# The last head pair's activations turned by TensorE instead of by the DMA, and one store per token block in the last chunk

## The chip, the cores and the metric

The kernel runs on one core of one Trainium2 chip. The metric is the device time of one execution in microseconds; the kernel before took 352.42 us (the median of three runs, 352.25 to 353.17). The profile shown further down is of one of these executions, with a span of 351.2 us and TensorE at its full clock throughout.

## What is computed

The reference is a causal attention with a forget gate for 8 batches of 8 heads, 576 tokens and head size 64, followed by a two-layer network with an exact GELU. The heads of one token, side by side, are its 512 inputs to the network.

```python
# attention: q, k, v (8, 8, 576, 64), f (8, 8, 576)
scores = scale * np.matmul(q, k.transpose(0, 1, 3, 2))
cum = np.cumsum(np.log(np.clip(f, 0.0001, 1.0)), axis=-1)
scores = np.where(causal, -1e9, scores + cum[:, :, :, None] - cum[:, :, None, :])
attn = softmax(scores)                      # written out in the reference
o = np.matmul(attn, v)
# network: x (4608, 512), w_in (512, 2048), w_out (2048, 512)
x = o.transpose(0, 2, 1, 3).reshape(B * S, H * D)
h = x @ w_in
g = 0.5 * h * (1.0 + erf(h / sqrt(2)))
out = g @ w_out                             # (4608, 512) f32
```

## The kernel before

The kernel works batch by batch. Of a batch's 576 tokens, 512 go through the network as a chunk of their own; the last 64 of every batch are gathered in `tails`, and these eight pieces make a ninth chunk, which is computed at the end. For a batch from 2 to 7 the stages are:

1. `attention(b)`: for each of four head pairs, four score tiles on TensorE, whose exponentials ScalarE takes. Between the score tiles, `take(fill, n)` puts n steps of the second matrix product of the batch before, so that TensorE has something to do while ScalarE works. `av(i)` multiplies the exponentials of pair i with v, and `normalize` writes `x` on VectorE.
2. `x`, which has tokens on the partitions, must be turned so that features lie on the partitions: `xT`. Batches 2 to 7 do this for each pair with one DMA transpose that SyncE issues (`x_dma`).
3. `gemm1(b, ffb)` multiplies a block of 128 columns of `w_in` with `xT` in four products (`kt` 0 to 3, one for each head pair), and ScalarE's GELU brings the result out of PSUM. There are 16 such blocks.

```python
    def to_xT(b, i, copy, pool=m_psum, tag="m", ps=None):      # on TensorE
        if ps is None:
            shape = [P, 2, 1024] if pool is s_psum else [P, XC]
            ps = pool.tile(shape, BF16, tag=tag, name="ps_x")
            if pool is s_psum:
                ps = ps[:, 0, 0:XC]
        for m in range(NBLK):                                  # NBLK = 5
            nc.tensor.transpose(
                ps[:, m * P : (m + 1) * P], x_of[b, i][:, m, :, :], ident_bf
            )
        copy(xT(b)[:, i, :], ps)

    def x_dma(b, i):                                           # by the DMA
        nc.sync.dma_start_transpose(
            xT(b)[:, i, :].rearrange("d (m p) -> d m p", p=P),
            x_of[b, i].rearrange("p m h d -> p (m h d)"),
        )

    def x_tail(b):
        nc.gpsimd.tensor_copy(tails[:, :, b * TL : (b + 1) * TL], xT(b)[:, :, XC - TL :])

    def gemm1(c, ffb, kts=range(4), ps=None, act=True):
        src = xT(c) if c < B else tails
        if ps is None:
            ps = m_psum.tile([P, TC], FP32, tag="m", name="ps1")
        for kt in kts:
            nc.tensor.matmul(ps, w_in_sb[:, kt, ffb * P : (ffb + 1) * P],
                             src[:, kt, 0:TC], start=(kt == 0), stop=(kt == n_dm - 1))
        if n_dm - 1 in kts and act:
            gelu(c, ffb, ps)                                   # ScalarE, g <- ps
        return ps
```

A step of the second product is either "n" (one product with all 128 rows of the array) or "r" (two products with 64 rows each, side by side). A plan has 64 steps for a batch.

```python
    PLAN = [
        (0, "o", 16 * "r"),
        (1, "m", 6 * "r" + "n" + 8 * "r" + "n"),
        (2, "m", 9 * "r" + "n" + 6 * "r"),
        (3, "s", 5 * "r" + 11 * "n"),
    ]
    # ... cut: PLAN_0, PLAN_1 (used in batch 2), gemm2_rows, which walks a plan ...

    FILL = [[7, 6, 3, 3], [1, 3, 3, 2], [1, 3, 3, 3], [1, 3, 3, 3], [6]]
    FILL_2 = [[8, 8, 8, 8], [8, 8, 4, 4], [4, 4, 4, 4], [4, 4, 4, 4], [6]]

    def attention(b):
        # ... cut: which fill ...
        for i in range(HP):                                    # HP = 4 head pairs
            for t in range(4):
                scores(b, i, t)
                take(fill, counts[i][t])
                if i and t == 1:
                    av(i - 1)
                    x_dma(b, i - 1)
                # ... cut: loads and transposes of the next batch's q, k, v ...
        take(fill, counts[HP][0])
        av(HP - 1)
        x_dma(b, HP - 1)
        take(fill, 999)                                        # what is left

        pss = [gemm1(b, ffb, (0, 1)) for ffb in range(2)]
        for ffb in range(2):
            gemm1(b, ffb, (2,), pss[ffb])
        more = s_psum.tile([P, 2, 512], FP32, tag="s", name="ps1")
        pss += [more[:, 0, :], more[:, 1, :]]
        gemm1(b, 2, (0, 1, 2), pss[2])
        for ffb in range(3):
            gemm1(b, ffb, (3,), pss[ffb])
        gemm1(b, 3, range(4), pss[3])
        if b + 1 < B:
            untangle(b + 1, 0)
            weigh_v(b + 1, 0)
        x_tail(b)

    # the main loop, after attention(b):
        for ffb in range(4, n_ff):                             # n_ff = 16
            gemm1(b, ffb)
            # ... cut: untangle (VectorE) and weigh_v (GpSimd) of the next batch ...
```

The first four blocks are thus ordered so that the products with the last pair (`kt` 3) come as late as they can. The pools `s_psum`, `o_psum` and `m_psum` have two buffers each; `more` is one buffer of `s_psum` with two banks.

The last chunk's stores (line 424) are made in `gemm2`, one for each batch that has 64 rows in the block of 128:

```python
                if c < B:
                    at = [(c * S + ts * P, 0, P)]
                else:
                    b0 = P // TL * ts
                    at = [(b * S + TC, (b - b0) * TL, TL) for b in range(b0, b0 + P // TL)]
                for row, p0, n in at:
                    (nc.scalar if p0 else nc.sync).dma_start(
                        out[row : row + n, c0:c1], ot[p0 : p0 + n, c0:c1]
                    )
```

Of the kernel before, what the change touches and what calls it, by code (L numbers as in the profile page):

```python
# [8 lines left out]
FP32 = mybir.dt.float32  # L9
# [5 lines left out]
P = 128  # L15
S = 576
D = 64
H = 8
HP = 4
NBLK = 5  # L20
K0 = [0, 128, 256, 384, 448]
TC = 512
# [30 lines left out]
def kernel(  # L53
# [10 lines left out]
    nc = tc.nc  # L64
    B = q.shape[0]
# [4 lines left out]
    n_ff = d_ff // P  # L70
    n_sub = TC // P
    XC = NBLK * P
    TL = S - TC
# [14 lines left out]
    s_psum = ctx.enter_context(tc.tile_pool(name="s_psum", bufs=2, space=PSUM))  # L88
    o_psum = ctx.enter_context(tc.tile_pool(name="o_psum", bufs=2, space=PSUM))
# [47 lines left out]
    for t, op, fill in (  # L137
# [4 lines left out]
            out=t[0:D],  # L142
            in_=t[0:D],
            compare_op=op,
            fill=fill,
# [89 lines left out]
    def untangle(b, i):  # L235

        for which, src in enumerate(tq_of[b]):
            for h in range(2):
                dst = (qT, kT)[which][i]
                rows = dst[h * D : (h + 1) * D, :].rearrange(  # L240
                    "d (p j two) -> d two p j", j=JT // 2, two=2
                )
                for odd in range(2):
                    nc.vector.tensor_copy(  # L244
                        rows[:, odd],
                        src[odd * D : (odd + 1) * D, 2 * i + h].rearrange(
                            "d j p -> d p j"
                        ),
                    )
# [3 lines left out]
    def weigh_v(b, i, eng=nc.gpsimd):  # L253

        if b not in vw_of:
            vw_of[b] = v_pool.tile([P, H, NBLK, D + 1], BF16, tag="vw", name=f"vw{b}")
        hs = slice(2 * i, 2 * i + 2)
        bh = b * H + 2 * i
        w = wT[:, :, bh : bh + 2].rearrange("p n h -> p h n")
        eng.tensor_tensor(  # L260
            vw_of[b][:, hs, :, 0:D],
            v_sb[:, hs, :, :],
            w.unsqueeze(3).to_broadcast([P, 2, NBLK, D]),
            Alu.mult,
        )
        eng.tensor_copy(vw_of[b][:, hs, :, D], w)
# [79 lines left out]
    def to_xT(b, i, copy, pool=m_psum, tag="m", ps=None):  # L346
# [5 lines that stand above are left out]
        for m in range(NBLK):  # L352
# [5 lines that stand above are left out]
    def x_dma(b, i):  # L358
# [7 lines that stand above are left out]
# [4 lines left out]
# [5 lines that stand above are left out]
            nc.tensor.matmul(  # L375
                ps,
                w_in_sb[:, kt, ffb * P : (ffb + 1) * P],
                src[:, kt, 0:TC],
                start=(kt == 0),
                stop=(kt == n_dm - 1),  # L380
            )
        if n_dm - 1 in kts and act:
            gelu(c, ffb, ps)
        return ps
# [9 lines left out]
    def gemm2(c):  # L394

        whole = (0, d_model)
        order = [(ts, kt, whole) for ts in range(n_sub) for kt in range(n_ff)]
        if c == B:
            order[-n_ff:] = [
                (n_sub - 1, kt, part)  # L400
                for part in ((0, 3 * P), (3 * P, d_model))
                for kt in range(n_ff)
            ]
        pss = {}
        for ts, kt, (c0, c1) in order:
            if kt == 0:
                pss[ts] = m_psum.tile([P, d_model], FP32, tag="m", name="ps2")
            nc.tensor.matmul(  # L408
                pss[ts][:, c0:c1],
                g_of[c][kt][:, ts * P : (ts + 1) * P],  # L410
                w_out_sb[:, kt, c0:c1],
                start=(kt == 0),
                stop=(kt == n_ff - 1),
            )
            if kt == n_ff - 1:
                ot = o_pool.tile([P, d_model], FP32, tag="ot", name="ot")
                nc.vector.tensor_copy(ot[:, c0:c1], pss[ts][:, c0:c1])  # L417
                if c < B:
                    at = [(c * S + ts * P, 0, P)]
                else:  # L420
                    b0 = P // TL * ts
                    at = [(b * S + TC, (b - b0) * TL, TL) for b in range(b0, b0 + P // TL)]
                for row, p0, n in at:
                    (nc.scalar if p0 else nc.sync).dma_start(
                        out[row : row + n, c0:c1], ot[p0 : p0 + n, c0:c1]
                    )
            yield


# [2 lines left out]
        (0, "o", 16 * "r"),  # L432
        (1, "m", 6 * "r" + "n" + 8 * "r" + "n"),
        (2, "m", 9 * "r" + "n" + 6 * "r"),
        (3, "s", 5 * "r" + 11 * "n"),
    ]

    PLAN_0 = [(2, "o", 16 * "r"), (3, "m", 14 * "r" + 2 * "n")]
# [1 line left out]
        (0, "m", 14 * "r" + 2 * "n"),  # L440
        (1, "m", 14 * "r" + 2 * "n"),
        (2, "m", 14 * "r" + 2 * "n"),
        (3, "s", 6 * "r" + 10 * "n"),
    ]

    def gemm2_rows(c, plan):
# [74 lines left out]
    def take(gen, n):  # L521
        for _ in range(n):
            if next(gen, "end") == "end":
                return
# [89 lines left out]

    FILL = [[7, 6, 3, 3], [1, 3, 3, 2], [1, 3, 3, 3], [1, 3, 3, 3], [6]]
    FILL_2 = [[8, 8, 8, 8], [8, 8, 4, 4], [4, 4, 4, 4], [4, 4, 4, 4], [6]]
    FILL_1 = [[0, 0, 0, 0], [0, 0, 0, 0], [2, 2, 2, 2], [2, 2, 2, 2]]

    def attention(b):


        fill = gemm2_third() if b == 2 else gemm2_rows(b - 1, PLAN)
        counts = FILL_2 if b == 2 else FILL

        def av(i):
            for h in range(2):
                attend(b, i, h, (0, 1, 2, 3, 4))
                normalize(b, i, h)  # L630

        for i in range(HP):
            for t in range(4):
                scores(b, i, t)
                take(fill, counts[i][t])
                if i and t == 1:
                    av(i - 1)
                    x_dma(b, i - 1)
                if t == 1 and i == 0:
                    load_v(b + 1)  # L640
                if b > 2 and t == 0 and i < 2:
                    transpose_dma(b + 1, 4 * i, 4 * i + 4)
                if b == 2 and t == 1 and i == 1:
                    transpose_dma(3, 0, 4)
                    transpose_dma(3, 4, 8)
        take(fill, counts[HP][0])
        av(HP - 1)
        x_dma(b, HP - 1)
        take(fill, 999)

        pss = [gemm1(b, ffb, (0, 1)) for ffb in range(2)]
        for ffb in range(2):
            gemm1(b, ffb, (2,), pss[ffb])
        more = s_psum.tile([P, 2, 512], FP32, tag="s", name="ps1")
        pss += [more[:, 0, :], more[:, 1, :]]
        gemm1(b, 2, (0, 1, 2), pss[2])
        for ffb in range(3):
            gemm1(b, ffb, (3,), pss[ffb])
        gemm1(b, 3, range(4), pss[3])
        if b + 1 < B:  # L660
            untangle(b + 1, 0)
            weigh_v(b + 1, 0)
        x_tail(b)

    def second_attention():

# [40 lines left out]
    for b in range(B):  # L707
        if b == 0:
            first_attention()
        elif b == 1:  # L710
            second_attention()
        else:
            attention(b)
        if b == 0:
            x_tail(0)
        for ffb in range(4, n_ff):
            gemm1(b, ffb)
            if b == 0:
                if ffb == 14:
                    for which in range(2):  # L720
                        transposes_first(1, 0, which, o_psum, "o")
                if ffb == 12:
                    weigh_v(1, 0)
                    load_w_out(0)
                    load_w_out(1)
                    weigh_v(1, 1)
                    load_qk_tokens(2, which="q")
            elif b + 1 < B:
                first, gap = (5, 3) if b == 1 else (0, 4)
                at, late = divmod(ffb - first, gap)  # L730
                if late == 0:
                    untangle(b + 1, at)
                if late == gap - 2:
                    weigh_v(b + 1, at)
                if ffb == (9 if b == 1 else 14):
                    load_qk_tokens(b + 2)
# [34 lines left out]
```

## Time and profile before

| | |
|---|---|
| median of 3 runs | 352.42 us |
| span of the profiled execution | 351.2 us |
| TensorE busy | 333.2 us (95%) |
| ScalarE busy | 211.1 us (60%) |
| VectorE busy | 184.2 us (52%) |
| GpSimd busy | 124.9 us (36%) |
| DMA transposes `xT<-x` | 24, 2.6 us from issue to landing (median) |
| DMA transposes of q and k | 24, 4.8 and 4.3 us |

In the profile, PE is TensorE's products and PEld its loads of weights, DVE is VectorE, ACT is ScalarE, POOL is GpSimd and SP is SyncE, which only issues transfers. "L375" is line 375 of the kernel: the products of `gemm1`. L466 are the fill steps, L408 the second product of batch 7 and of the last chunk, L289 the scores, L320 the products with v, L353 the transposes on TensorE, L356 the copies of their results, L359 the DMA transposes of `x`, L392 the GELU, L333 and L334 the normalization, L244 the copies that sort the next batch's transposed q and k, L260 the weighting of v, and L365 the copy into `tails`. A wait is put down to the operation that ended last before the waiting one could start.

TensorE is busy nearly without pause, and from batch 3 on the stages repeat every 36.78 us. Batch 3's attention ends near 143 us of the span, batch 7's near 290 us; the last chunk's first product starts at 319.3 us and its second at 333.5 us.

### The profile page before, as it was taken

To read this page: it belongs to the slowest core of one execution; us is meant where nothing else is said; L and a number is where in the kernel's file an instruction comes from. 1 tells how busy PE (TensorE), PEld (TensorE's weight loads), DVE (VectorE), ACT (ScalarE), POOL (GpSimd) and SP (SyncE) were. 2 spreads that over 40 slices of the span, in tenths; PEclk is the share of its full clock that TensorE was granted. 3 is DMA by queue.
4 is the path that set the end of the run, shared out by engine and by line. 5 is a ranking of instruction groups with operands and counts; after the bars stand their busy time and mean duration, and the time that the engine had idled before them with its cause. 6 is when DMAs were issued, how large, how long until landed. Compare 5 with 4: busy or idle time off the path is not lost.

```text
span 351.2 us, 7855 instructions
## 1 busy us (share of the span) xinstructions
PE 333.2 (95%) x3180; PEld 172.5 (49%) x3180; DVE 184.2 (52%) x417; ACT 211.1 (60%) x296; POOL 124.9 (36%) x256
## 2 busy tenths in 40 slices
PE   8799999999997999899989999899989998999995
PEld 3574555445542456445644564346534553444443
DVE  4770456924449735894479446955596551011011
ACT  5976786774533787268736873687457764603600
POOL 8480763037326044623454243614350430000000
PEclk9999999999999999999999999999999999999999
DMA  7999999969993999299937896489600131011013
GB/s 111 182 186 194 194 162 150 161 154 171 228 174 105 152 194 173 87 134 167 202 100 98 167 208 112 75 150 210 156 30 2 51 99 49 0 62 61 0 30 92
DMA packets 104628, 44.18 MB, mean 126 GB/s; under 512 B 83408, under 2 KB 100048, under 8 KB 104592
## 3 DMA queue, kind: packets, MB, share of 16 engines
q1 hardware_dynamic: 87296, 29.52, 43.2%
q0 software_dynamic: 16896, 13.63, 26.8%
q8 instruction: 25, 0.41, 0.5%
q10 hardware_dynamic: 400, 0.52, 0.4%
q14 instruction: 11, 0.09, 0.1%
HBM read 36.85 MB, written 9.44 MB: 132 GB/s over the span
## 4 chain that ended last, share of the span: by engine, by line
PE 88%; ACT 5%; DMA 2%; POOL 2%; DVE 2%; issue 1%; POOLq 0%; ACTq 0%
PE ps L375 34%; PE ps L466 27%; PE o L320 8%; PE ps L408 8%; PE s L289 7%; ACT g L392 3%; PE ps L501 2%; ACT e L299 2%; DMA k<-in_k_dram 2%; POOL q L107 1%; DMA xT<-x 1%; PE ps_f L206 1%; DVE x L334 1%; POOL k L107 1%; PE ps_x L353 1%
## 5 line engine op out<-in xcount | busy, mean ns | idle before, releaser
L392 ACT ACTIVATE g<-ps 128x512 bf16<-128x512 f32 x144 | 84.0, 597 | 90.0 <-PE ps L375 90.0
L375 PE MATMUL ps<-xT,w_in_sb 128*128 128x512 bf16 x512 | 113.8, 379 | 8.6 <-ACT g L392 7.4
L299 ACT ACTIVATE e<-s 128x896 bf16<-128x896 f32 (+2 forms) x128 | 101.3, 836 | 28.8 <-PE s L289 26.1
L466 PE MATMUL ps<-w_out_sb,g 64*128 64x512 bf16 (+1 forms) x744 | 109.2, 377 | 0.0
L375 PEld LDWEIGHTS <-w_in_sb 128*128 128x128 bf16 x576 | 55.9, 98 | 77.5 <-issue 12.7
L301 POOL TENSOR_SCALAR_AFFINE_SELECT e<-e 128x256 bf16<-128x256 bf16 (+1 forms) x135 | 49.5, 385 | 103.9 <-ACT e L299 103.6
L466 PEld LDWEIGHTS <-g 64*128 64x128 bf16 (+1 forms) x744 | 41.8, 94 | 41.6 <-issue 11.9
L260 POOL TENSOR_TENSOR vw<-v_sb,wT 128x640 bf16<-128x640 f32 x31 | 40.0, 1289 | 33.1 <-DMA v_sb<-in_v_dram 23.5
L289 PE MATMUL s<-qT,kT 64*128 64x320 bf16 (+4 forms) x384 | 45.8, 276 | 3.4 <-ACT e L299 2.7
L474 DVE COPY ot<-ps 128x512 f32<-128x512 f32 x26 | 18.0, 692 | 53.7 <-PE ps L466 53.7
L244 DVE COPY qT<-tq 64x288 bf16<-64x288 bf16 x96 | 43.1, 449 | 1.4
L244 DVE COPY kT<-tk 64x288 bf16<-64x288 bf16 x96 | 37.9, 394 | 1.6
L320 PEld LDWEIGHTS <-e 128*128 128x128 bf16 x960 | 34.7, 98 | 5.8 <-issue 0.6
L320 PE MATMUL o<-vw,e 128*128 128x65 bf16 x960 | 36.8, 194 | 0.3 <-POOL e L301 0.2
L334 DVE TENSOR_TENSOR x<-o,r 128x320 bf16<-128x320 f32 x64 | 31.5, 492 | 2.2
L417 DVE COPY ot<-ps 128x512 f32<-128x512 f32 (+2 forms) x9 | 5.7, 633 | 50.2 <-PE ps L408 50.2
L289 PEld LDWEIGHTS <-kT 64*128 64x128 bf16 x384 | 19.5, 94 | 23.0 <-issue 9.3
L408 PE MATMUL ps<-w_out_sb,g 128*128 128x512 bf16 (+2 forms) x144 | 28.0, 355 | 0.0
L333 DVE RECIPROCAL r<-o 128x5 f32<-128x5 f32 x64 | 12.1, 190 | 24.4 <-PE o L320 24.3
L408 PEld LDWEIGHTS <-g 128*128 128x128 bf16 x144 | 13.5, 98 | 14.5
L476 DVE TENSOR_TENSOR ot<-ot,ps 128x512 f32<-128x512 f32 x26 | 17.9, 687 | 1.4
L375 PE MATMUL ps<-tails,w_in_sb 128*128 128x512 bf16 x64 | 14.3, 378 | 0.0
(64 smaller groups left out, 139.7 us busy)
## 6 DMA issues: line engine op xcount, KB each, us to landing
out_dram<-ot SPq DMA_DIRECT2D x32, 256.0 KB, 2.4
v_sb<-in_v_dram SPq DMA_DIRECT2D x24, 256.0 KB, 5.0
q<-in_q_dram POOLq DMA_DIRECT2D x6, 576.0 KB, 6.1
k<-in_k_dram POOLq DMA_DIRECT2D x6, 576.0 KB, 8.6
v_sb<-in_v_dram SPq DMA_DIRECT2D x22, 128.0 KB, 5.0
w_in_sb<-in_moe_w_in_dram POOLq DMA_DIRECT2D x4, 512.0 KB, 7.2
w_out_sb<-in_moe_w_out_dram POOLq DMA_DIRECT2D x4, 512.0 KB, 8.7
q<-in_q_dram POOLq DMA_DIRECT2D x4, 144.0 KB, 5.1
```

Of the source, the lines that this page charges most:

```text
L244: nc.vector.tensor_copy(rows[:, odd], src[odd * D : (odd + 1) * D, 2 * i + h].rearrange("d j p -> d p j"),)
L260: eng.tensor_tensor(vw_of[b][:, hs, :, 0:D], v_sb[:, hs, :, :], w.unsqueeze(3).to_broadcast([P, 2, NBLK, D]), Alu.mult,)
L289: nc.tensor.matmul(to, *ab, start=half < 0, stop=half == 1 or not masked)
L299: nc.scalar.activation(et[:, :, z:c], st[:, :, z:c], Act.Exp, scale=scale)
L301: nc.gpsimd.affine_select(out=et[:, :, c0 + z : c0 + P], in_=et[:, :, c0 + z : c0 + P], compare_op=Alu.is_ge, fill=0.0, base=z, pattern=[[ ...
L320: nc.tensor.matmul(o[:, m, :], e_of[b, i, t][:, h, c : c + P], vw_of[b][:, 2 * i + h, n, :], start=(n == 0), stop=(n == m),)
L334: nc.vector.tensor_tensor(x_of[b, i][:, :, h, :], o[:, :, 0:D], r.unsqueeze(2).to_broadcast([P, NBLK, D]), Alu.mult,)
L375: nc.tensor.matmul(ps, w_in_sb[:, kt, ffb * P : (ffb + 1) * P], src[:, kt, 0:TC], start=(kt == 0), stop=(kt == n_dm - 1),)
L392: nc.scalar.activation(g_of[c][ffb], ps, Act.Gelu)
L408: nc.tensor.matmul(pss[ts][:, c0:c1], g_of[c][kt][:, ts * P : (ts + 1) * P], w_out_sb[:, kt, c0:c1], start=(kt == 0), stop=(kt == n_ff - 1),)
L466: nc.tensor.matmul(banks[r], g_of[c][kt][rows, ts * P : (ts + 1) * P], w_out_sb[rows, kt, :], start=kt == (steps.index("r") if r else 0), ...
L474: nc.vector.tensor_copy(ot, banks[1])
```

## The change

For batches 2 to 7, the last head pair's `x` is turned by five transposes on TensorE into PSUM and one VectorE copy into `xT`. To give VectorE time to write `x` and to copy the result, six of the last eight fill steps are put between the products with v and the transposes, and two behind them; two steps move ahead of the products with v. In batch 2 the third pair is turned in this way too. With `xT` complete sooner, the special order of the first four `gemm1` blocks is dropped: all 16 blocks run in one loop, each with its four products in a row, on the two buffers of `m_psum`. Sorting and weighting for the next batch start inside this loop, and the copy into `tails` is issued ahead of the weighting.

Apart from that, a token block of the last chunk is stored by one transfer with two groups of 64 rows, issued by SyncE, instead of one on SyncE and one on ScalarE. It saves an issue and frees ScalarE's queue of stores.

```diff
                 if c < B:
-                    at = [(c * S + ts * P, 0, P)]
+                    to = out[c * S + ts * P : c * S + (ts + 1) * P, c0:c1]
                 else:
                     b0 = P // TL * ts
-                    at = [(b * S + TC, (b - b0) * TL, TL) for b in range(b0, b0 + P // TL)]
-                for row, p0, n in at:
-                    (nc.scalar if p0 else nc.sync).dma_start(
-                        out[row : row + n, c0:c1], ot[p0 : p0 + n, c0:c1]
-                    )
+                    to = out.rearrange("(b s) d -> b s d", s=S)[
+                        b0 : b0 + P // TL, TC:S, c0:c1
+                    ]
+                nc.sync.dma_start(to, ot[:, c0:c1])

     PLAN = [ ...
-        (3, "s", 5 * "r" + 11 * "n"),
+        (3, "s", 7 * "r" + 9 * "n"),
     PLAN_1 = [ ...
-        (3, "s", 6 * "r" + 10 * "n"),
+        (3, "s", 8 * "r" + 8 * "n"),

-    FILL = [[7, 6, 3, 3], [1, 3, 3, 2], [1, 3, 3, 3], [1, 3, 3, 3], [6]]
-    FILL_2 = [[8, 8, 8, 8], [8, 8, 4, 4], [4, 4, 4, 4], [4, 4, 4, 4], [6]]
+    FILL = [[7, 6, 3, 3], [1, 3, 3, 2], [1, 3, 3, 3], [1, 3, 3, 3], [8]]
+    FILL_2 = [[8, 8, 8, 8], [8, 8, 4, 4], [4, 4, 4, 4], [4, 4, 4, 4], [8]]

     def attention(b): ...
                     av(i - 1)
-                    x_dma(b, i - 1)
+                    if i < HP - 1 or b > 2:
+                        x_dma(b, i - 1)
     ...
         take(fill, counts[HP][0])
+        if b == 2:
+            to_xT(b, HP - 2, nc.vector.tensor_copy, s_psum, "s")
         av(HP - 1)
-        x_dma(b, HP - 1)
+        take(fill, 6)
+        to_xT(b, HP - 1, nc.vector.tensor_copy, o_psum, "o")
+        x_tail(b)
         take(fill, 999)
-
-        pss = [gemm1(b, ffb, (0, 1)) for ffb in range(2)]
-        for ffb in range(2):
-            gemm1(b, ffb, (2,), pss[ffb])
-        more = s_psum.tile([P, 2, 512], FP32, tag="s", name="ps1")
-        pss += [more[:, 0, :], more[:, 1, :]]
-        gemm1(b, 2, (0, 1, 2), pss[2])
-        for ffb in range(3):
-            gemm1(b, ffb, (3,), pss[ffb])
-        gemm1(b, 3, range(4), pss[3])
-        if b + 1 < B:
-            untangle(b + 1, 0)
-            weigh_v(b + 1, 0)
-        x_tail(b)

     # main loop
-        for ffb in range(4, n_ff):
+        for ffb in range(0 if b > 1 else 4, n_ff):
             gemm1(b, ffb)
```

## The prediction

> **What bounds the kernel now.** I began with the page, went on to TensorE's waits from 65 us on (batch 2 starts a little later), and then read the timeline at the end of one batch's attention. First the page's first section, then the waits (waiting operation, what ended the wait, us in total, how often, longest):
>
> ```profile
> PE 333.2 (95%) x3180; PEld 172.5 (49%) x3180; DVE 184.2 (52%) x417; ACT 211.1 (60%) x296; POOL 124.9 (36%) x256
> ```
>
> ```profile
> PE ps L375 <- ACT g L392: 7.4, 6, 1.2
> PE ps L375 <- DMA xT<-x: 1.2, 1, 1.2
> ```
>
> TensorE is the bound, and after 65 us its products stand idle in seven places only: six times on a GELU, once in each of batches 2 to 7, and once on a DMA transpose. Both are in the block of code that the change replaces. The stretches by stage say the same of one whole period (us, then busy time of PE, PEld, DVE, ACT and POOL):
>
> ```profile
> 143.29:180.07 36.78, 35.54 (x347) 18.50 (x346) 24.55 (x56) 24.47 (x34) 15.25 (x31) 1.00 0.83 144
> ```
>
> 36.78 less 35.54 is 1.24 us, so the one wait of 1.23 us is all of the idle time in a period. The timeline around it (start, us, then [idle before, what ended it]):
>
> ```profile
> 140.02 1.11 PE L320 MATMUL o<-vw,e 128*128 128x65 bf16 x30
> ...
> 140.97 2.32 PE L466 MATMUL ps<-w_out_sb,g 128*128 128x512 bf16 x10
> ...
> 141.55 0.49 DVE L334 TENSOR_TENSOR x<-o,r 128x320 bf16<-128x320 f32 x1
> ...
> 143.13 2.75 PE L375 MATMUL ps<-xT,w_in_sb 128*128 128x512 bf16 x12
> ...
> 145.49 1.57 ACT L392 ACTIVATE g<-ps 128x512 bf16<-128x512 f32 x3 [5.22 <-PE ps L375]
> ...
> 147.11 2.75 PE L375 MATMUL ps<-xT,w_in_sb 128*128 128x512 bf16 x12 [1.23 <-ACT g L392]
> ```
>
> Twelve `gemm1` products run, which are blocks 0, 1 and 2; then TensorE waits until three GELUs are through, and block 3 starts. Blocks 2 and 3 are the two halves of `more`, and block 2's GELU is emitted ahead of block 3's products. So block 3 waits for a read of the other half of its buffer. It is not the DMA that costs the time here: `kt` 3 ran without a gap.
>
> The wait is worth more than 1.23 us. Products overlap in the pipeline: ten fill steps from 140.97 to 143.13 make a pitch of 0.216 us, though each lasts 0.38 us. The twelfth product started near 143.13 + 11 × 0.216 = 145.51, and the next could have started at 145.72. It started at 147.11: **1.39 us lost per batch**.
>
> Batch 2 has this wait and the one for the DMA:
>
> ```profile
> 104.77 1.03 PE L375 MATMUL ps<-xT,w_in_sb 128*128 128x512 bf16 x4
> 106.96 2.14 PE L375 MATMUL ps<-xT,w_in_sb 128*128 128x512 bf16 x8 [1.16 <-DMA xT<-x]
> ...
> 110.33 1.89 PE L375 MATMUL ps<-xT,w_in_sb 128*128 128x512 bf16 x8 [1.23 <-ACT g L392]
> ```
>
> Without any wait the thirteenth product would start at 104.77 + 12 × 0.216 = 107.36. It started at 110.33, so 2.97 us are lost there.
>
> **What the Trainium skill says.** "TensorE: Matmul & The Clock Gate", section "Back-to-back issue gap", gives an isolated gap of about N/2.4 + 2.5 ns, that is 216 ns for 512 columns and 56 ns for 128. The trace agrees: 216 ns here, and 58 ns for a transpose below. The same section's 131 ns for 512 columns in a sustained stream is not seen in this trace. "VectorE: DVE Perf Modes", section "The three transpose paths", lists 390 ns for a 128x128 bf16 transpose on TensorE and 1309 ns by the DMA. Here five by the DMA take 2.6 us from issue to landing, and TensorE's start one after the other far faster than 390 ns, so I use the trace. "SBUF — State Buffer", section "SBUF: two separate sides", says that VectorE and GpSimd share one port pair under an exclusive lock in certain operations. The trace agrees: four copies of L244 took 3.52 us from 144.66, beside GpSimd's weighting, and 1.34 us from 157.91, when GpSimd was idle.
>
> **The change, part by part.** What five transposes cost TensorE is in the second batch's last pair, which this kernel already does so:
>
> ```profile
> 59.25 0.45 PE L353 MATMUL ps_x<-ident_bf,x 128*128 128x128 bf16 x5
> ...
> 59.54 1.24 PE L375 MATMUL ps<-xT,w_in_sb 128*128 128x512 bf16 x5
> ...
> 59.74 0.49 DVE L356 COPY xT<-ps_x 128x640 bf16<-128x640 bf16 x1 [0.55 <-PE ps_x L353]
> ```
>
> From the first transpose to the next product are 59.54 − 59.25 = 0.29 us (58 ns each). The copy starts 0.49 us after the first transpose, and `xT` is there 0.98 us after it.
>
> *Removed:* the 1.39 us, if no new wait takes its place. *Added:* 0.29 us of transposes. *Moved:* two fill steps across the products with v, at no cost, for an r step's pair takes one pitch too (12 products in 1.29 us by the chain of waits). Now the three places where a new wait could arise, counted from the first product with v (140.02 before).
>
> - *Transposes wait for `x`.* Before, the last `x` was written at 141.55 + 0.49 = 142.04, which is 2.02. The 30 products end their turn at 0.95 (140.97), six fill steps bring it to 0.95 + 6 × 0.216 = 2.25. So 0.2 us to spare.
> - *`kt` 3 of block 0 waits for the copy.* The copy ends at 2.25 + 0.98 = 3.23. TensorE gets there after transposes (0.29), two steps (0.43) and three products (0.65): 3.62. So 0.4 us to spare. The fill's own copies come behind it in VectorE's order.
> - *Block 2 waits for block 0's GELU* to give back its `m_psum` buffer: four products take 0.864 us, a GELU 0.60 us. The twelve later blocks already run so, 52 products in 11.38 us with no wait in the trace.
>
> So a batch from 3 to 7 gains 1.39 − 0.29 = 1.10 us: five of them, **5.5 us**.
>
> *Batch 2* turns two pairs, 0.58 us. VectorE has more ahead of the last `x`: the fill's copy (99.82 before, 0.69), its sum (0.69), the first pair's copy (0.49), then two normalizations (1.35, as from 140.69 to 142.04): 99.82 + 3.22 is about 103.1. TensorE reaches the transposes at 99.71 + 0.43 + 0.29 + 0.95 + 1.30 = 102.7, plus perhaps 0.3 for going from 64 rows to 128 and back once more, so 0 to 0.4 us is lost. The waits for DMA and GELU go. 2.97 − 0.58 − 0.4 is about **1.9 us**.
>
> *The end.* The last copy ends at 347.50 + 0.29 = 347.79. Its two stores land 2.0 us (SyncE) and 2.2 us (ScalarE) after issue. "DMA: Bandwidth & Descriptors", section "Issuing engines are not separate DMA queues", has it that issuing from several engines saves only issue time; a SyncE issue here takes 0.47 us and the one before it starts at 347.2, so it hardly delays the last. One store instead of two ends with SyncE's: about **0.15 us**.
>
> The sum is 5.5 + 1.9 + 0.15 = 7.55 us, and 352.42 − 7.55 = **344.9 us**, 2.1% less.
>
> **The rivals.**
>
> *A wait moves in for the one removed.* The margins, 0.2 and 0.4 us, are thin, and if VectorE is late by half a microsecond each batch loses 0.3 to 0.5 us. For it: the copy is in VectorE's order ahead of work that used to be there. Against: `x` is written as before, and VectorE stood idle 0.45 us ahead of the normalization. Result: 346.5 to 347.5 us.
>
> *The next batch's preparation becomes the bound.* The weighting's first part now starts after the `tails` copy, some 2.8 us later than 141.27, so more of VectorE's sorting runs beside GpSimd at a third of its speed. The sorting ended at 159.25, and SyncE's transposes of q and k wait for it, then v's loads and `x`'s transposes behind them. The next attention starts 1.6 us sooner against the sorting. Against: by my count sorting ends at the same distance from the products with v (19.1 against 19.2 us), the third pair's transpose still lands over 1 us ahead of `kt` 2, and v's loads are issued by 166, for a weighting at 178. Result if wrong: about 346 to 348 us.
>
> *The transfer was hidden anyway, and only the transposes are paid:* then 2 us slower, 354. The waits on L392 speak against it; they depend on the order of code that is dropped.
>
> **Range and chances.** The mechanism is read directly, so slower is nearly out. The errors lie on the side of less gain: each 0.2 us per batch is 1.2 us in all. I take 344.0 to 347.0. The 2% line is at 345.4, only half a microsecond above my number, so faster by over 2% gets 0.6 and within 2% 0.39.
>
> **What would show it.** In the profile after: no wait of L375 on L392 and none on the DMA after 65 us; 35 more transposes in L353 (75), and 17 instead of 24 DMA transposes of `x`; a period of 35.7 us instead of 36.78; TensorE's loss in batch 2 about 1 us; the last stores landing some 2.0 to 2.2 us after issue. A new line of L353 waiting on L334, or L375 on L356, each six times, would be the first rival; a wait of L289 on L244 or of L320 on L260 the second. The prediction is wrong if the period stays above 36.2 us.

## The result and the profile after

The changed kernel takes 357.9 us (median of 4 runs, 357.61 to 359.12) against 352.68 us: a ratio of 1.0154, with a 95% interval of 1.0126 to 1.0183. It is 5.2 us slower, where I had foretold 7.5 us less.

TensorE did what the prediction said. The stretches by stage of the changed kernel (us, then busy time of PE, PEld, DVE, ACT and POOL, granted clock, DMA share, GB/s), with the last row from the end of TensorE's last product to the end:

```profile
141.55:177.22 35.67, 35.66 (x354) 18.76 (x353) 25.38 (x58) 24.69 (x34) 15.20 (x31) 1.00 0.79 144
177.22:212.88 35.66, 35.65 (x354) 18.75 (x353) 25.37 (x58) 24.69 (x34) 15.19 (x31) 1.00 0.77 144
339.90:355.60 15.70, 0.00 (x0) 0.00 (x0) 0.29 (x1) 0.00 (x0) 0.00 (x0) 0.64 0.12 44
```

A period is 35.67 us instead of 36.78, and TensorE is idle for 0.01 us of it. After 65 us of the span no product waits for anything that the profile shows. The timeline at the end of an attention shows the new order (start, us):

```profile
139.38 1.46 PE L465 MATMUL ps<-w_out_sb,g 128*128 128x512 bf16 x6
140.68 0.44 PE L353 MATMUL ps_x<-ident_bf,x 128*128 128x128 bf16 x5
140.96 0.59 PE L465 MATMUL ps<-w_out_sb,g 128*128 128x512 bf16 x2
141.39 13.98 PE L375 MATMUL ps<-xT,w_in_sb 128*128 128x512 bf16 x64
```

Six fill steps, five transposes in 0.28 us, two fill steps, then all 64 products without a gap. TensorE's last product ends at 339.90; before it ended at 347.48. So TensorE is 7.58 us ahead, and the program ends 4.4 us later all the same: 355.6 against 351.2.

The third row above holds the loss: 15.70 us in which TensorE does nothing and the DMA is busy to 0.12. VectorE's last copy ends at 340.21, so 15.4 us lie between it and the end. In the kernel before they were 3.4 us:

```profile
347.79:351.20 3.41, 0.00 (x0) 0.00 (x0) 0.01 (x1) 0.00 (x0) 0.00 (x0) 0.97 0.30 77
```

The granted clock falls only in this end: it is 1.00 up to 344 and 0.50 from 345 on, when TensorE has had no product for 4 us. In every stage before it was 1.00, so the mean of 0.984 over the whole span follows from the long end and does not cause it. SyncE's waits name what the end waits for, in the changed kernel and in the kernel before (us in total, times, longest; both lines are the end of the program):

```profile
SPq L756 <- DMA out_dram<-ot: 8.7, 1, 8.7
```

```profile
SPq L766 <- DMA out_dram<-ot: 1.4, 2, 1.2
```

The stores of the last chunk take the time. Two stretches while such stores run, in the changed kernel and in the kernel before:

```profile
342.00:344.00 2.00, 0.00 (x0) 0.00 (x0) 0.00 (x0) 0.00 (x0) 0.00 (x0) 1.00 0.13 51
```

```profile
339.00:340.00 1.00, 1.00 (x7) 0.46 (x5) 0.00 (x0) 0.00 (x0) 0.00 (x0) 1.00 0.93 246
```

The last two columns are what the reader is to see. A share of 0.13 is two of 16 DMA engines (2/16 = 0.125), and they move 51 GB/s; before, the share is that of nearly all engines, and they moved 246 GB/s. At 51 GB/s a block of 256 KB takes 5.1 us, but a new block comes every 3.45 us. The stores pile up: at that rate all 1.05 MB need 20.6 us, and in the trace they flow from near 331.5 to near 353.5, the first microseconds more slowly (31 GB/s from 332 to 334). The last issue shows it too. It held SyncE for 4.83 us, the others for about 0.5:

```profile
340.25 4.83 SPq L425 DMA_DIRECT2D out_dram<-ot  x1
```

### The profile page after: what moved, and what is told of

Read it like the earlier page. It is cut to its first block, busy times and chain, and to the rows that moved or that the text cites. A ratio compares the mean times of both kernels' runs of the same rounds, so it can differ in the third digit from the quotient of the medians.

```text
span 355.6 us, 7929 instructions
## 1 busy us (share of the span) xinstructions
PE 334.2 (94%) x3227; PEld 174.6 (49%) x3227; DVE 186.7 (52%) x424; ACT 212.4 (60%) x296; POOL 124.5 (35%) x256
## 4 chain that ended last, share of the span: by engine, by line
PE 87%; POOL 2%; DVE 2%; ACT 2%; DMA 2%; issue 1%; POOLq 0%; ACTq 0%; DVEq 0%
PE ps L375 35%; PE ps L465 26%; PE o L320 8%; PE ps L408 8%; PE s L289 7%; PE ps L500 2%; ACT e L299 2%; DMA k<-in_k_dram 2%; PE ps_x L353 1%; DVE x L334 1%; POOL q L107 1%; PE ps_f L206 1%; POOL k L107 1%; DVE r L333 0%; DVE xT L356 0%
## 5 line engine op out<-in xcount | busy, mean ns | idle before, releaser
L392 ACT ACTIVATE g<-ps 128x512 bf16<-128x512 f32 x144 | 85.4, 597 | 81.1 <-PE ps L375 81.1
L375 PE MATMUL ps<-xT,w_in_sb 128*128 128x512 bf16 x512 | 112.5, 379 | 0.0
L244 DVE COPY qT<-tq 64x288 bf16<-64x288 bf16 x96 | 48.6, 506 | 1.4
L244 DVE COPY kT<-tk 64x288 bf16<-64x288 bf16 x96 | 33.0, 343 | 1.6
L334 DVE TENSOR_TENSOR x<-o,r 128x320 bf16<-128x320 f32 x64 | 31.5, 492 | 2.4 <-DVE r L333 0.2
```

The lines of the kernel that those rows point to most:

```text
L244: nc.vector.tensor_copy(rows[:, odd], src[odd * D : (odd + 1) * D, 2 * i + h].rearrange("d j p -> d p j"),)
L334: nc.vector.tensor_tensor(x_of[b, i][:, :, h, :], o[:, :, 0:D], r.unsqueeze(2).to_broadcast([P, NBLK, D]), Alu.mult,)
L392: nc.scalar.activation(g_of[c][ffb], ps, Act.Gelu)
```

## Experiments

Theory A, formed on this trace: one transfer is spread over as many DMA engines as its destination's outermost dimension has entries. Two groups of 64 rows, whose addresses lie a batch apart, make that dimension 2. Theory B: SyncE alone can't carry the stores. Theory C: a destination of three dimensions, or one transfer in place of two, is slow in itself. The end is counted from the end of VectorE's last copy to the end of the span.

### The TensorE part alone

```diff
# the changed kernel; cut: `at` in place of `to`, as in the kernel before
-                nc.sync.dma_start(to, ot[:, c0:c1])
+                for row, p0, n in at:
+                    (nc.scalar if p0 else nc.sync).dma_start(
+                        out[row : row + n, c0:c1], ot[p0 : p0 + n, c0:c1]
+                    )
```

> The changed kernel with the stores of the kernel before (one transfer for each group of 64 rows, SyncE and ScalarE). If the loss lies in the stores, the TensorE part stands alone: the profile after has TensorE done 7.6 us sooner (339.90 against 347.48), and the end costs the old 3.4 us, so about 345 us, with the granted clock back at 1.00. If the TensorE part itself were slower (the granted clock of 0.984), it stays near 357.

Measured: 345.15 us against 352.94, a ratio of 0.9785 (0.9739 to 0.9831); the clock is 1.000 and the end 343.2 − 339.81 = 3.4 us. The TensorE part gives what was expected, and the granted clock was no cause: it is back at 1.000 with the same TensorE part.

### The store part alone

```diff
# the kernel before, with the changed kernel's store; cut: the loop over `at`, and `to` in its place
-                    (nc.scalar if p0 else nc.sync).dma_start(...)
+                nc.sync.dma_start(to, ot[:, c0:c1])
```

> The kernel before with the new stores alone. From the last copy's end to the end of the span the profiles show 3.4 us before and 15.4 us after; if that is the stores' doing, whatever the rest of the kernel is, this takes 352.7 + 12.0 = 364.7 us. If the loss needs both parts, it stays near 353.

Measured: 364.36 us, a ratio of 1.0316 (1.0261 to 1.037). The end:

```profile
348.51:363.10 14.59, 0.00 (x0) 0.00 (x0) 0.00 (x1) 0.00 (x0) 0.00 (x0) 0.58 0.12 45
```

14.6 us with the same share of 0.12, and nothing of the TensorE part in the kernel; the last issue held SyncE for 4.91 us here too. So neither part needs the other for its effect: −7.8 and +11.4 us. Their sum, +3.6, falls short of the +5.2 measured for both; the kernel before alone ranged from 351.68 to 354.59 on this chip, so I don't read more into it.

### Two transfers, both on SyncE

```diff
# the changed kernel; cut: `at` in place of `to`, as in the kernel before
-                nc.sync.dma_start(to, ot[:, c0:c1])
+                for row, p0, n in at:
+                    nc.sync.dma_start(
+                        out[row : row + n, c0:c1], ot[p0 : p0 + n, c0:c1]
+                    )
```

> The changed kernel with two transfers of 64 rows each per block, both issued by SyncE. Theory A, the one transfer runs on two of the 16 DMA engines since its outermost dimension is 2: each of these two transfers has 64 rows outermost, so all engines work, and it takes about 345 us, at most 0.5 us more than with ScalarE's share. Theory B, SyncE's queue alone can't carry the stores: near 357 us.

Measured: 346.86 us, a ratio of 0.9829 (0.9783 to 0.9876); the end is 346.1 − 341.68 = 4.4 us. Theory B is out: the same bytes from the same queue pass at once when each transfer has 64 rows outermost. The end is 1.0 us longer than with ScalarE's share, where I had allowed 0.5: SyncE's last issue ends 2.05 us after the last copy, and with ScalarE's share both queues were done after 0.80. The median is 1.7 us longer (346.86 against 345.15), so some 0.7 us lie ahead of the end; what they are is not shown.

### One transfer with 4, 8 or 16 groups

The last chunk's rows are put in another order in `tails`, so that a block of 128 rows holds 4 groups of 32, 8 of 16, or 16 of 8 rows; every row still goes to its own place in the output. For 16:

```diff
# the changed kernel
-        nc.gpsimd.tensor_copy(tails[:, :, b * TL : (b + 1) * TL], xT(b)[:, :, XC - TL :])
+        nc.gpsimd.tensor_copy(
+            tails.rearrange("p k (s b) -> p k s b", b=B)[:, :, :, b],
+            xT(b)[:, :, XC - TL :],
+        )
-                    to = out.rearrange("(b s) d -> b s d", s=S)[
-                        b0 : b0 + P // TL, TC:S, c0:c1
-                    ]
+                    n = P // B
+                    to = out.rearrange("(b s) d -> s b d", s=S)[
+                        TC + ts * n : TC + (ts + 1) * n, :, c0:c1
+                    ]
```

> The changed kernel with the rows of the last chunk in another order (token first, batch second), so that a block's one SyncE transfer has 16 groups of 8 rows in the destination in place of 2 groups of 64. Theory A (as many DMA engines as the outermost dimension has entries): all 16, the end back at about 3.3 us, in all about 345 us. Theory C, a destination of three dimensions is slow in itself, or one transfer in place of two: near 357 us.

> As with 16 groups, but the last chunk's rows are ordered so that a block's one SyncE transfer has 4 groups of 32 rows in the destination. Theory A (as many DMA engines as groups): with 2 groups the DMA share was 0.13 and the rate 51 GB/s, so here a share of 0.25 and about 102 GB/s while a store runs; 256 KB then take 2.6 us, less than the 3.45 us between two blocks, so nothing piles up, and from the last copy's end to the span's end I expect 4.5 to 5.5 us (15.4 with 2 groups, 3.9 with 16). Theory C, a three-dimensional destination costs by its descriptors: as slow as with 2 groups, about 15 us.

> As before with 8 groups of 16 rows. Theory A: a DMA share of 0.5 and about 205 GB/s while a store runs, and an end of 3.9 to 4.3 us, so within half a microsecond of 16 groups. Theory C: about 15 us again.

A stretch of full flow in each, with 4, 8 and 16 groups:

```profile
337.50:338.50 1.00, 1.00 (x9) 0.61 (x7) 0.00 (x0) 0.00 (x0) 0.00 (x0) 1.00 0.27 104
```

```profile
341.50:342.00 0.50, 0.00 (x0) 0.00 (x0) 0.00 (x0) 0.00 (x0) 0.00 (x0) 1.00 0.52 192
```

```profile
342.00:342.50 0.50, 0.00 (x0) 0.00 (x0) 0.00 (x0) 0.00 (x0) 0.00 (x0) 1.00 0.92 296
```

| groups in one transfer | DMA share, GB/s | the end, us | median, us | ratio to the kernel before |
|---|---|---|---|---|
| 2 (the change) | 0.13, 51 | 15.4 | 357.9 | 1.0154 (1.0126 to 1.0183) |
| 4 | 0.27, 104 | 8.2 | 349.82 | 0.9896 (0.9854 to 0.9938) |
| 8 | 0.52, 192 | 4.8 | 346.62 | 0.9804 (0.9755 to 0.9854) |
| 16 | 0.92, 296 | 3.9 | 347.06 | 0.9829 (0.9782 to 0.9877) |

The share follows the number of groups, twice for twice, as theory A has it. The packets give the number exactly. While the last chunk is stored, the changed kernel's queue carries (packets, MB, share of 16 engines):

```profile
q1 hardware_dynamic: 650, 1.05, 9.4%
```

With 4, 8 and 16 groups they are 660, 680 and 720. In each, 640 packets carry the data; the others have 4 bytes, and for each of the five transfers there are 2, 4, 8 or 16 of them, one for each group. The ten transfers of 64 rows from SyncE have 800 packets, which is 16 small ones each. The data packets are the same in number and size in all of these kernels, so their size is not the cause. Nor is it whether a group's rows adjoin: with 16 groups each row lies a batch from the next one of its group, with 2, 4 and 8 they adjoin.

Theory C is out: all four are one transfer with three dimensions, and with 16 groups the end falls to 3.9 us. All three expectations for the end were too short: 3.3 for 16 groups, 4.5 to 5.5 for 4, and 3.9 to 4.3 for 8. With 4 groups, 104 GB/s holds only in the later part of each store; the first one begins with 1.5 us of much slower flow (49, then 12, then 8 GB/s in the half microseconds from 331.5), at shares of 0.40, 0.28 and 0.06. With 8 groups the flow begins slowly too (33 GB/s at a share of 0.43 from 331.5). From first to last byte the mean with 4 groups is about 70 GB/s, so stores pile up a little there too. What that slow start is, these runs do not show. With 16 groups the median is 1.9 us above that of the TensorE part with the old stores (347.06 against 345.15, on one chip). The end explains 0.5 of them; the rest lies ahead of it and stays open.

### What the TensorE part gains by

Two kernels take the two halves of that part separately. In the first, the kernel before keeps its DMA transposes and its order, but the GELUs of blocks 2 and 3 are emitted later:

```diff
# the kernel before
         for ffb in range(3):
-            gemm1(b, ffb, (3,), pss[ffb])
-        gemm1(b, 3, range(4), pss[3])
+            gemm1(b, ffb, (3,), pss[ffb], ffb < 2)
+        gemm1(b, 3, range(4), pss[3], False)
+        gelu(b, 2, pss[2])
+        gelu(b, 3, pss[3])
```

> The kernel before (DMA transposes, its stores, its order of the first four blocks), with the GELUs of blocks 2 and 3 emitted after block 3's products. If what the TensorE part gains is only the wait for a GELU on the other half of a buffer, six times 1.39 us come back without any transpose on TensorE: 352.9 - 8.3 = 344.6 us, up to 346 if later blocks wait a little for ScalarE. If the DMA transposes limit it, it stays above 350 us.

Measured: 347.04 us, a ratio of 0.9822 (0.9772 to 0.9872). In batches where no DMA transpose came late:

```profile
218.49:253.98 35.49, 34.74 (x341) 18.50 (x347) 24.60 (x57) 24.37 (x35) 14.87 (x31) 1.00 0.91 149
253.98:289.46 35.48, 34.73 (x340) 18.49 (x346) 23.43 (x54) 24.35 (x35) 12.24 (x28) 1.00 0.18 50
```

35.48 us is even less than the change's 35.67. So the wait on the other half of a buffer was the cost: emitting these two GELUs later gives 1.30 us per batch back. Of the time itself I had expected 344.6, at most 346. In the profiled execution, the slowest of the four, batch 2's blocks started some 4 us later than in the kernel before (108.72 against 104.77), and another batch waited 0.5 us for a DMA transpose.

The second has the plain loop of the change, but all its `x` turned by the DMA, with the stores of before:

```diff
# the changed kernel, stores of before; cut: the third pair of batch 2, also back to the DMA
-        take(fill, 6)
-        to_xT(b, HP - 1, nc.vector.tensor_copy, o_psum, "o")
-        x_tail(b)
+        x_dma(b, HP - 1)
         take(fill, 999)
+        x_tail(b)
```

> The changed kernel with the stores of before and all its x turned by the DMA again: the plain loop of 16 blocks without the transposes on TensorE. The last pair is written 2.02 us after the first product with v and its transfer lands 2.6 us later; block 0 reaches its fourth product at 0.95 + 8 x 0.216 + 0.65 = 3.33 us, so it waits 1.35 us and saves 0.29 us of transposes: 1.06 us per batch slower than with TensorE's transposes, about 2.3 us in batch 2, in all about 352 us. If the transposes were hidden anyway, it is the fastest, about 343 us.

Measured: 354.85 us (352.55 to 357.75), a ratio of 1.0042 (1.0 to 1.0084), more than the expected 352 and widely spread; the profiled execution took 352.87. Its period and TensorE's longest wait after 65 us:

```profile
146.70:183.56 36.86, 34.80 (x343) 18.46 (x349) 25.81 (x58) 24.69 (x34) 15.09 (x32) 1.00 0.81 144
```

```profile
PE ps L375 <- DMA xT<-x: 8.4, 7, 1.6
```

36.86 is 1.19 us above 35.67, where I had worked out 1.06 (by the terms given it is 1.00, since 2.02 + 2.6 − 3.33 is 1.29 and not 1.35). The plain loop is worth its gain only with `xT` complete sooner: the transposes on TensorE cost 0.29 us and take away a DMA wait of 1.2 us, which by the pitch of the products is worth 1.36 us.

### Which way is the best

Side by side on one chip: the TensorE part, the late GELUs, and a mixture, with the changed way in batch 2 alone, where the kernel before waits for the DMA, and late GELUs in batches 3 to 7. All have the stores of before.

```diff
# the mixture, from the changed kernel with the stores of before
+        if b == 2:
+            ... the changed way, then return
+        ... the way before, with the GELUs of blocks 2 and 3 emitted last
-        for ffb in range(0 if b > 1 else 4, n_ff):
+        for ffb in range(0 if b == 2 else 4, n_ff):
```

> The stores of before; in batch 2 the changed way (two pairs turned by TensorE, the plain loop of 16 blocks), in batches 3 to 7 the way before (all pairs turned by the DMA, first four blocks in the special order) with the GELUs of blocks 2 and 3 emitted late. The period was 35.67 us with TensorE's transposes and 35.48 us with late GELUs, so five batches should gain 5 x 0.19 = 0.95 us on the changed TensorE part alone: about 344.2 us. If a DMA transpose comes late now and then, as in two batches of the run with late GELUs, that is eaten up: 345 us or more.

> The changed TensorE part with the stores of before once more, beside the other two on the same chip: 345.2 us.

> The kernel before with late GELUs once more. Each of six batches saves 1.30 us by the period of 35.48: 352.9 - 7.8 = 345.1 us where no DMA transpose comes late; 347 us, as measured, where some do.

| | median, us | ratio to the kernel before |
|---|---|---|
| mixture | 345.77 (344.85 to 347.3) | 0.9791 (0.9763 to 0.982) |
| TensorE part | 345.67 (345.41 to 348.96) | 0.9804 (0.9767 to 0.984) |
| late GELUs | 346.29 (344.88 to 347.71) | 0.9801 (0.9772 to 0.9831) |

They can't be told apart; the mixture's 0.95 us does not show in the medians. In the kernel with late GELUs TensorE still waits for a DMA transpose now and then:

```profile
PE ps L375 <- DMA xT<-x: 1.0, 2, 0.7
```

All three beat both the kernel before and the change as it was given. The smallest edit of them is the late GELUs, which need no transpose on TensorE at all.

## Why the prediction was wrong, point by point

- *The bound and the loss per batch: right.* I read 1.39 us lost per batch from the pitch of the products; with late GELUs 1.30 us came back, the rest being small new gaps.
- *1.10 us per batch from the change: right.* The period fell from 36.78 to 35.67 us. The three margins held: the transposes started at 140.68, or 2.25 after the first product with v (138.43), as worked out, and the profile puts no product's wait down to L334, L356 or L392.
- *Batch 2, 1.9 us: right.* The terms give 1.99, which I put as about 1.9; 2.03 was measured: the first score product of batch 3 starts at 119.62, before at 121.65. With five periods of 1.11 us less that makes the whole 7.58 us. The transposes started at 103.05, where I had 102.7 plus up to 0.4, and here they did wait for `x`, which was written at 102.99.
- *The end, 0.15 us gained: this step failed.* It was written as "One store instead of two ends with SyncE's", on the ground of the issue time alone, and it took the landing time of 2.0 us of a 64-row transfer over to a transfer of another shape. The term is +12.0 us (15.4 less 3.4), not −0.15. The transfer's shape, which I had in the diff, sets how many DMA engines work on it, and two of 16 could not keep up with a block every 3.45 us. With the other terms as they stood, 7.4 − 12.0 makes the program 4.6 us slower; the spans of the two profiled executions differ by 4.4 us, the medians by 5.2.
- *The rivals:* none of the three came. I looked for a new wait on TensorE, VectorE, GpSimd and in the loads. The stores, which the title names beside the TensorE part, got one paragraph and no rival. "Slower is nearly out" rested on the TensorE part alone.

One sign of the first rival, a new line of L353 waiting on L334, did appear, though the rival did not. TensorE's loads of `x` waited, in the whole span of the kernel before and then of the changed one (us in total, times, longest):

```profile
PEld L353 <- DVE x L334: 1.6, 3, 0.6
```

```profile
PEld L353 <- DVE x L334: 2.9, 9, 0.6
```

The six new ones are one for each of batches 2 to 7. From batch 3 on they cost nothing, since the products of the fill steps were still running: a period has 0.01 us without a product. The sign did not tell a load's wait from a product's.

The page that I cited for the issuing engines states the rule I lacked. The Trainium skill, "DMA: Bandwidth & Descriptors", section "Why a DMA increments its semaphore by 16 and not by 1", says that a transfer uses the largest number of engines up to 16 that divides the slowest dimension of both access patterns. For an output pattern of 2 × 64 × 512 that is 2. The runs agree at 2, 4, 8 and 16, with shares of 0.13, 0.27, 0.52 and 0.92 and as many small packets for each transfer.

## What to carry to other kernels

Before two transfers are merged into one, look at the outermost dimension of the merged pattern: it sets how many DMA engines share the work, and here a 2 cost 12 us where a saved issue was to gain 0.15. If the bytes can be laid out so that this dimension is 16, one transfer comes near to two: the end was 3.9 us against 3.4 with two issuers and 4.4 with two transfers from SyncE. That it beats two issuers is not shown; the program with 16 groups took 1.9 us more.

A wait on a buffer can come from its other half; a later emission of the reader may give back what a new data path would. Here it gave 1.30 us per batch against 1.11.

A change of several parts is priced part by part, and a part without a measured number of its own kind, here a store with that shape, has no known price. The last transfers of a program deserve it most: here no other work lay behind them to hide their 12 us.

## What the runs showed that I had not expected

- The flow of one transfer grew with the groups in its destination: 51, 104, 192 and 296 GB/s for 2, 4, 8 and 16, which is some 26 GB/s for each group with 2 and 4, 24 with 8 and 18.5 with 16.
- Stores that pile up can hold up their issuer as well: with two engines at work the last store's issue took 4.83 and 4.91 us on SyncE instead of about 0.5. With 4 groups, where they pile up less, it took about 0.6.
- With GpSimd's four weightings in a row, four of VectorE's sorting copies took 5.04 us from 142.95, against 1.34 us alone, and no product on TensorE waited for them.
